# A mixture-of-experts stage whose second part is listed from a graph of tasks

## The chip, the cores and the metric

The kernel runs on one core of a Trainium2 chip. The metric is device time in microseconds (us) of the whole program, the median of several executions. Engines are named as in the profile: PE multiplies matrices, DVE and ACT work on vectors, POOL is GpSimd, SP issues most of the loads. Each engine takes its instructions strictly in the order in which they were written for it; an instruction that waits holds up everything behind it on that engine.

## The reference, cut to what matters

Three layers follow each other. A retention (8 x 8 heads of 576 x 64) gives 4608 tokens of 512 numbers. A dense layer maps them by `h = x @ w_in`, `(h - tanh(h)) @ w_out` with 2048 hidden columns. Then each token goes to one of eight experts, and an expert takes exactly 576 tokens:

```
logits = x @ w_gate
order = np.argsort(-flat)            # all (token, expert) pairs, best first
for idx in order:
    tok, e = int(idx) // E, int(idx) % E
    if assigned[tok] >= 0 or counts[e] >= cap: continue
    assigned[tok] = e; counts[e] += 1
for e in range(E):
    h = np.maximum(x[assigned == e] @ w1[e], 0.0)
    out[assigned == e] = h @ w2[e]
```

## The kernel before, in words

The first part (retention and dense layer, `phase_ab`) is listed by a planner of its own, the class `Tasks`; it ends at about 985 us and is the same in both kernels. The second part, `phase_c`, is what the change rewrites. It runs eight rounds. A round has two halves.

Routing (`route(r)`) finds which expert fills up next and which 576 tokens it gets. It is a long chain of small DVE operations with a small PE product after every few of them: six threshold searches (a compare `cmp`, L839 or L925; a product L930 or L934; `ca` L938; products L949 and L950; a reduce, a transpose, a count `pi` L957 to L960), then `GG` (L969, product L973), `X` and the expert's number `ei` (L985 to L990, products L995 and L996), then places and indices: the scan `sc` L1006, `zl` L1013, `zh` L1014, `b1` L1018 (printed `b`), `A` L1021, `R` (one half on ACT, L1019, one on DVE, L1023), product L1027, `im`, `ix`, product L1045, `idx` L1050. Round r+1 starts from the state that round r leaves: `epen`, `v`, `tpen`, `own`, `rem`.

An expert (`experts(r)`, called E0 to E7 here) gathers its tokens by index on POOL (`xg`, L1097, five tiles), turns them on PE (`tp`, L1112), splits them into a high part `xh` (ACT, L1114) and a low part `xl` (DVE, L1115); both weights are loaded by SP (`ws`, L1063 and L1068) and split in the same way into `w1h`, `w2h` (ACT, L1074) and `w1l`, `w2l` (POOL, L1075). The first layer has eight slices f of 24 PE products (L1158), each slice followed by `hh` (ACT, L1167) and three DVE operations for `hl` (L1171); the two PSUM banks of a slice are free again when these are done, and there are four such banks. The second layer has 112 PE products (L1189) in five token tiles (t0, t4, t1, t2, t3), and per tile an output `o` (ACT, L1197, L1199) that POOL scatters (L1201).

What sets the order of all this: `experts` writes its products one by one and calls `tick` after each pair (`TK1` = 0.24) or each one (`TK2` = 0.213). `tick` moves one clock on and lets three threads (routing, first-layer weights, tokens) write their next piece when the distance that they last yielded has passed. The distances are constants:

```
Y_TR, Y_CA, Y_H, Y_GG, Y_X, Y_Z, Y_R, Y_IX = 2.0, 0.85, 0.5, 2.9, 2.7, 4.2, 1.8, 2.7
YS = 0.82, 0.85
```

Everything between two yields is written in one piece. So `b1` and the ACT half of `R` are written together, whatever ACT has still to do for the first layer; and `w2h` of slice f is written behind `hh` of slice f.

Of the kernel before, what the change touches and what calls it, by code (L numbers as in the profile page):

```python
# [41 lines left out]
def lat(a, b):  # L42

    if a == b:
        return 0.0
    if "dma" in (a, b):
        return 0.9 if a == "dma" else 1.2
    return 0.2 if "tensor" in (a, b) else 0.15

# [23 lines left out]
class Tasks:  # L73
# [17 lines left out]
    def run(self, free):  # L91
# [31 lines left out]
        assert left == 0  # L123

# [607 lines left out]


Y_TR, Y_CA, Y_H, Y_GG, Y_X, Y_Z, Y_R, Y_IX = 2.0, 0.85, 0.5, 2.9, 2.7, 4.2, 1.8, 2.7

YS = 0.82, 0.85
TK1 = 0.24
TK2 = 0.213

# [9 lines left out]
def phase_c(tc, ctx, w1, w2, rtf, rti, rth, rtb, x2d, L, out):  # L749
# [69 lines left out]
    key = SB["key"].bitcast(I32)  # L819

    def best(r):

        V.tensor_reduce(SB["m"], VN[r], axis=AX.X, op=OP.max)
        MT[r] = rt([128, NCOL], F32, "mt")
        V.tensor_tensor(MT[r], SB["m"], tpen, op=OP.min)

    def keys(r):

        n1 = SB["n1"].bitcast(I32)
        HI[r] = rt([128, NCOL], I32, "hi")  # L830
        mb = MT[r].bitcast(I32)
        V.tensor_scalar(n1, mb, c31, c80, op0=OP.arith_shift_right, op1=OP.bitwise_or)
        V.tensor_tensor(key, mb, n1, op=OP.bitwise_xor)
        V.tensor_scalar(HI[r], key, c16, cff, op0=OP.arith_shift_right, op1=OP.bitwise_and)
        compare0(r, HI[r])

    def compare0(r, src):
        CM[r] = rt([128, NCOL, 32], BF16, "cmp32")
        V.tensor_tensor(CM[r], bc(src, 2, 32), bc(SB["s0"], 1, NCOL), op=OP.is_ge)  # L839

    def route(r):


        fast = r < FAST
        q0 = rt([128, NCOL, E], F32, "q0")
        e0 = SB["e0"].rearrange("p (c e) -> p c e", e=E)
        m8 = rt([128, NCOL], F32, "m8")
        P = rt([128, NCOL, E], BF16, "P")
        if r == 0:
            best(0)  # L850
            yield 0.75
            keys(0)
            yield 2.0
        v, m, mt = VN.pop(r), SB["m"], MT.pop(r)

        def proposals():
            V.tensor_tensor(q0, v, bc(m, 2, E), op=OP.is_equal)
            yield 0.5
            V.tensor_tensor(e0, q0, bc(SB["w8"], 1, NCOL), op=OP.mult)
            yield 0.5  # L860
            V.tensor_reduce(m8, e0, axis=AX.X, op=OP.max)
            yield 0.5
            V.tensor_tensor(P, e0, bc(m8, 2, E), op=OP.is_equal)
# [5 lines left out]
        GG = rt([128, NCOL, 2, E], BF16, "GG")  # L869
        gg = SB["gg"].rearrange("p (c a) -> p c a", a=2)  # L870
        if r < E - 1:

            hi = HI.pop(r)
            lo = rt([128, NCOL], I32, "lo")
            hs = SB["hs"]
            lf = rt([128, NCOL], F32, "lf")
            T = pi = None
            for half in range(2):
                src = hi
                if half:  # L880
                    ts = rt([128, 1], F32, "ts")
                    V.tensor_scalar(ts, pi, T, 65536.0, op0=OP.add, op1=OP.mult)
                    V.scalar_tensor_tensor(lf, hs, ts, lo, op0=OP.subtract, op1=OP.add)
                    src = lf
                D = None
                for s, (shift, J) in enumerate(STEPS):
                    if s == 0:
                        if half:
                            compare0(r, src)
                        cmp_ = CM.pop(r)  # L890
                        if fast:

                            if not half:
                                src = rt([128, NCOL], F32, "hf")
                                nc.gpsimd.tensor_copy(out=src, in_=hi)
                            D = fp.tile([128, KC, CAP], F32R, tag="xl", name="D", bufs=2)
                            D = D.rearrange("p k t -> p (k t)")[:, :NCOL * 64].bitcast(F32)
                            D = D.rearrange("p (c j) -> p c j", c=NCOL)
                            nc.gpsimd.tensor_tensor(D, bc(src, 2, 64), bc(F["s2"], 1, NCOL), op=OP.subtract)
                            src = lf if half else hi  # L900
                        if not half:
                            yield from proposals()
                            V.tensor_scalar(lo, key, cff, None, op0=OP.bitwise_and)
                            V.tensor_scalar(hs, hi, 65536.0, None, op0=OP.mult)
                            places()
                    elif s == 2 and fast:
                        cmp_ = rt([128, NCOL, J], BF16, "cmp64")
                        V.tensor_scalar(cmp_, D, T, pi, op0=OP.subtract, op1=OP.is_ge)
                        T2 = rt([128, 1], F32, "T")
                        V.tensor_tensor(T2, T, pi, op=OP.add)  # L910
                        T = T2
                    else:
                        cmp_ = rt([128, NCOL, J], BF16, f"cmp{J}")
                        thr = SB["thr"][:, :J]
                        if s == 1:
                            V.tensor_scalar(thr, F["s1"], pi, None, op0=OP.add)
                            T = pi
                        else:
                            V.tensor_scalar(thr, F["s2"], T, pi, op0=OP.add, op1=OP.add)
                            T = rt([128, 1], F32, "T")  # L920
                            V.tensor_copy(out=T, in_=thr[:, :1])
                        for j in range(0, J, 32):
                            if j:
                                yield 1.3
                            V.tensor_tensor(cmp_[:, :, j:j + 32], bc(src, 2, 32), bc(thr[:, j:j + 32], 1, NCOL), op=OP.is_ge)  # L925
                    yield (1.4 if half == 0 and s == 0 else Y_TR + 1.3) + Y_H * (half == 1 and s == 0)
# [9 lines left out]

# [3 lines left out]
                    yield Y_CA + 0.5 * J / 32  # L940


                    nj, nc_ = J // 32, 1 if fast else 4
                    pd = ps_r(8 * nj * nc_)
                    for i in range(nj):
# [4 lines left out]
                        nc.tensor.matmul(o[:, :E], H16["one"], rn, start=False, stop=True)  # L950
                    dm = rt([128, nj], F32, f"dm{nj}")
# [3 lines left out]
                    if not fast:  # L955
                        d8 = rt([128, nj, E], F32, f"d8{nj}")
                        V.tensor_reduce(d8, pd.rearrange("p (j c e) -> p j e c", j=nj, e=E), axis=AX.X, op=OP.add)  # L957
                    V.tensor_reduce(dm, d8, axis=AX.X, op=OP.max)
                    V.transpose(tr.rearrange("p (i j) -> p i j", j=32), bc(dm, 2, 32))
                    V.scalar_tensor_tensor(tr[:, 1:], tr[:, 1:], 0.0, SB["c"][:, s:s + 1].to_broadcast([128, J - 1]),  # L960
                                           op0=OP.is_ge, op1=OP.mult, accum_out=pi)
            V.tensor_scalar(gg[:, :, 0], lf, T, pi, op0=OP.subtract, op1=OP.is_gt)
            V.tensor_scalar(gg[:, :, 1], lf, T, pi, op0=OP.subtract, op1=OP.is_ge)
        else:
            yield from proposals()
            places()
            for a in range(2):
                V.tensor_scalar(gg[:, :, a], mt, -0.5 * BIG, None, op0=OP.is_gt)
        V.tensor_tensor(GG, bc(P, 2, 2), bc(gg, 3, E), op=OP.mult)  # L969
        yield Y_GG  # L970
# [4 lines left out]
        nc.tensor.matmul(pg[:, :16], H16["one"], rz.rearrange("p a e -> p (a e)"), start=False, stop=True)  # L975
        nn = rt([128, 2, E], F32, "nn")
        fw = rt([128, E], F32, "fw")
        mx = rt([128, 1], F32, "mx")
        V.tensor_reduce(nn, pg.rearrange("p (c a e) -> p a e c", c=12, a=2), axis=AX.X, op=OP.add)
        V.scalar_tensor_tensor(fw, nn[:, 1, :], 0.0, SB["w8"], op0=OP.is_ge, op1=OP.mult)  # L980
        V.tensor_reduce(mx, fw, axis=AX.X, op=OP.max)

        X = rt([128, 2, NCOL], BF16, "X")
        tk = rt([128, NCOL], F32, "tk")
        V.scalar_tensor_tensor(tk, m8, mx, gg[:, :, 0], op0=OP.is_equal, op1=OP.mult)  # L985
        V.scalar_tensor_tensor(X[:, 0, :], own, mx, tk, op0=OP.is_equal, op1=OP.add)
# [9 lines left out]
        nc.tensor.matmul(pt[:, :72], B["tri"], X72, start=True, stop=True)  # L996
        if r < E - 1:
            se = rt([128, E], F32, "se")
            V.tensor_scalar(se, SB["w8"], mx, None, op0=OP.is_equal)
            V.scalar_tensor_tensor(epen, se, -2 * BIG, epen, op0=OP.mult, op1=OP.add)  # L1000
            VN[r + 1] = rt([128, NCOL, E], F32, "v")
            V.tensor_tensor(VN[r + 1], L, bc(epen, 1, NCOL), op=OP.min)
        pos = SB["pos"]
        vd = rt([128, 72], F32, "vd")
        pb = rt([128, NCOL], F32, "pb")
        V.tensor_tensor_scan(sc[:, 1:73], one, pt[:, 72:], 0.0, op0=OP.mult, op1=OP.add)  # L1006
        V.tensor_tensor(pos, pt[:, :72], sc[:, 0:72], op=OP.add)
# [299 lines left out]
```

## Time and profile before

| | |
|---|---|
| median of 3 runs | 1521.57 us (1519.9 to 1521.99) |
| the profiled execution | 1526.22 us, its span 1524.0 us |
| PE busy, share of the span | 1448.0 us, 95% |
| DVE, ACT, POOL busy | 71%, 51%, 36% |
| mean granted PE clock over the span | 0.981 |
| first products of E0 to E7 start at | 1041.55, 1107.28, 1167.51, 1228.89, 1293.21, 1353.10, 1414.21, 1467.45 us |

PE is the engine that sets the time: the span can shrink only where PE stands idle or runs at a lower clock. Its 95% is an average, so the table of stages is read for the stretches where PE was not busy, and the list of waits for what ended the idle time.

### The profile page before, as it was taken

To read this page: it belongs to the slowest core of one execution; us is meant where nothing else is said; L and a number is where in the kernel's file an instruction comes from. 1 tells how busy PE (TensorE), PEld (TensorE's weight loads), DVE (VectorE), ACT (ScalarE), POOL (GpSimd) and SP (SyncE) were. 2 spreads that over 40 slices of the span, in tenths; PEclk is the share of its full clock that TensorE was granted. 3 is DMA by queue.
4 is the path that set the end of the run, shared out by engine and by line. 5 is a ranking of instruction groups with operands and counts; after the bars stand their busy time and mean duration, and the time that the engine had idled before them with its cause. 6 is when DMAs were issued, how large, how long until landed. Compare 5 with 4: busy or idle time off the path is not lost.

```text
span 1524.0 us, 26099 instructions
## 1 busy us (share of the span) xinstructions
PE 1448.0 (95%) x9499; PEld 1271.1 (83%) x9500; DVE 1075.9 (71%) x2683; ACT 779.3 (51%) x1616; POOL 541.6 (36%) x487
## 2 busy tenths in 40 slices
PE   7999999999999999999999999928999999999998
PEld 5788888898989888989888998817788788887987
DVE  5777757787888878787878787777676766766210
ACT  6899965555565646565555555512333323424321
POOL 2555631222221213222212222234535626446442
PEclk9999999999999999999999999959999999999999
DMA  8432132111111111202011100112432433426311
GB/s 280 153 118 93 59 124 80 63 42 63 42 63 43 44 62 38 68 22 84 21 63 42 65 1 21 38 63 83 136 117 81 135 96 103 132 75 198 102 59 39
DMA packets 48609, 122.42 MB, mean 80 GB/s; under 512 B 6624, under 2 KB 13408, under 8 KB 48224
## 3 DMA queue, kind: packets, MB, share of 16 engines
q1 hardware_dynamic: 41184, 99.80, 19.4%
q0 software_dynamic: 6144, 19.93, 4.1%
q8 instruction: 75, 1.23, 0.3%
q10 hardware_dynamic: 1152, 1.02, 0.2%
q14 instruction: 54, 0.44, 0.1%
HBM read 101.85 MB, written 18.87 MB: 79 GB/s over the span
## 4 chain that ended last, share of the span: by engine, by line
PE 75%; ACT 9%; DVE 6%; issue 4%; POOL 3%; DMA 2%; SPq 0%; POOLq 0%; ACTq 0%; DVEq 0%
PE x L490 22%; PE h L427 22%; PE ff L1189 12%; PE ff L1158 11%; PE pb L291 2%; PE pb L358 2%; PE pb L370 1%; ACT wst L213 1%; DMA wst<-in_wio 1%; ACT wst L218 1%; ACT t L440 1%; PE tp L1112 1%; PE pb L306 1%; POOL w2l L1075 1%; ACT S L437 1%
## 5 line engine op out<-in xcount | busy, mean ns | idle before, releaser
L471 POOL TENSOR_TENSOR gl<-t,gh 128x384 fp32r<-128x384 f32 x192 | 197.0, 1026 | 632.8 <-ACT gh L468 563.9
L427 PE MATMUL h<-xh,w0h 128*128 128x384 f32 x704 | 238.5, 339 | 2.0 <-DVE t L457 1.9
L437 ACT ACTIVATE S<-h 128x384 f32<-128x384 f32 x192 | 93.2, 486 | 283.4 <-PE h L427 283.4
L427 PE MATMUL h<-xh,w0l 128*128 128x384 f32 x704 | 236.7, 336 | 0.0
L490 PE MATMUL x<-w1h,gh 128*128 128x512 f32 x576 | 231.2, 401 | 3.2 <-ACT gh L468 2.4
L490 PE MATMUL x<-w1l,gh 128*128 128x512 f32 x576 | 226.7, 393 | 0.2 <-DVE w1l L238 0.2
L490 PE MATMUL x<-w1h,gl 128*128 128x512 f32 x576 | 217.8, 396 | 1.3 <-POOL gl L471 0.8
L451 DVE SCALAR_TENSOR_TENSOR t<-t,S 128x384 f32<-128x384 f32 x192 | 114.2, 595 | 140.7 <-ACT t L440 140.0
L531 DVE SCALAR_TENSOR_TENSOR junk<-x2r,wg 128x512 f32<-128x512 f32 x240 | 167.0, 696 | 5.1
L427 PE MATMUL h<-xl,w0h 128*128 128x384 f32 x704 | 151.6, 336 | 0.3 <-DVE xl L414 0.3
L427 PEld LDWEIGHTS h<-xh,w0h 128*128 128x128 f32 x704 | 131.9, 187 | 11.6 <-DVE t L457 3.5
L1075 POOL TENSOR_TENSOR w2l<-ws,w2h 128x512 fp32r<-128x512 f32 x64 | 82.5, 1290 | 164.5 <-ACT w2h L1074 164.5
L427 PEld LDWEIGHTS h<-xh,w0l 128*128 128x128 f32 x704 | 132.1, 188 | 7.1
L490 PEld LDWEIGHTS x<-w1h,gl 128*128 128x128 f32 x576 | 108.3, 189 | 28.8 <-POOL gl L471 5.7
L1189 PE MATMUL ff<-w2h,hh 128*128 128x512 f32 x320 | 128.1, 400 | 3.1 <-DVE hl L1171 2.0
L490 PEld LDWEIGHTS x<-w1h,gh 128*128 128x128 f32 x576 | 108.1, 188 | 26.5 <-ACT gh L468 3.8
L457 DVE COPY_PREDICATED t<-m,h 128x384 f32<-128x384 uint16 x192 | 114.6, 597 | 21.3 <-ACT m L446 2.6
L1189 PE MATMUL ff<-w2l,hh 128*128 128x512 f32 (+1 forms) x320 | 128.0, 400 | 0.6 <-POOL w2l L1075 0.6
L440 ACT ACTIVATE t<-S,bias 128x384 f32<-128x384 f32 x192 | 118.1, 615 | 17.1 <-POOL gl L471 1.1
L427 PEld LDWEIGHTS h<-xl,w0h 128*128 128x128 f32 x704 | 125.6, 188 | 0.9 <-DVE xl L414 0.9
L490 PEld LDWEIGHTS x<-w1l,gh 128*128 128x128 f32 x576 | 108.3, 188 | 17.7 <-DVE w1l L238 0.5
L1158 PE MATMUL ff<-xh,w1h 128*128 128x288 f32 x512 | 115.4, 304 | 6.3 <-DVE hl L1171 5.5
(212 smaller groups left out, 2936.5 us busy)
## 6 DMA issues: line engine op xcount, KB each, us to landing
ws<-in_w SPq DMA_DIRECT2D x128, 256.0 KB, 2.8
ain<-in_qkv SPq DMA_DIRECT2D x36, 768.0 KB, 4.1
wst<-in_wio SPq DMA_DIRECT2D x32, 512.0 KB, 3.6
x2d<-x2r SPq DMA_DIRECT2D x33, 256.0 KB, 2.0
w1h<-in_qkv SPq DMA_DIRECT2D x12, 192.0 KB, 4.4
w1l<-in_qkv SPq DMA_DIRECT2D x12, 192.0 KB, 3.7
w0h<-in_qkv SPq DMA_DIRECT2D x12, 192.0 KB, 4.6
w0l<-in_qkv SPq DMA_DIRECT2D x12, 192.0 KB, 5.3
```

The source lines that it names most:

```text
L291: nc.tensor.matmul(PSA[k][a][:, chunk(c)], kt[r, chunk(c)], q[r, chunk(c)], start=True, stop=True)
L427: nc.tensor.matmul(h[:, :TB], w[0][f][:, hp, :], x, start=i == 0, stop=i == 11)
L437: nc.scalar.activation(S, h, AF.Square, scale=KSC)
L440: nc.scalar.activation(AT[s][2], AT[s][1], AF.Square, bias=bias[:, 0:1])
L451: nc.vector.scalar_tensor_tensor(t, t, PA - PB * PB / 4, S, op0=OP.add, op1=OP.mult)
L457: nc.vector.copy_predicated(t, m.bitcast(U16), h)
L471: nc.gpsimd.tensor_tensor(G[s][1], TT.pop(s), G[s][0].bitcast(F32), op=OP.subtract)
L490: nc.tensor.matmul(X2[n][i], g[:, i * 128:i * 128 + 128], w, start=(f == 0 and g is gh and w is wh), stop=(f == NF - 1 and g is gl))
L531: nc.vector.scalar_tensor_tensor(j, r, 1.0, wg[e // 4][:, e % 4, :], op0=OP.mult, op1=OP.mult, accum_out=L[:, c, e:e + 1])
L1075: nc.gpsimd.tensor_tensor(l, s, h.bitcast(F32), op=OP.subtract)
L1158: nc.tensor.matmul(ps[u], w[:, k, :], x[:, k, 288 * u:288 * u + 288], start=i == 0, stop=i == 11)
L1189: nc.tensor.matmul(o, h, w, start=f == 0 and i == 0, stop=f == 7 and i == len(prods) - 1, skip_group_check=t == 4)
```

## The change: what it does

A new class `Flow` lists the second part. Every instruction, or small group of them, is a task with an engine, a duration in us, an urgency (the fourth argument, higher first) and the tasks that it has to wait for; buffers are such dependencies too. `Flow.run` steps through the tasks in the order of their planned times, and writes on each engine the most urgent one that is ready. `route` yields one engine and one duration per operation in place of distances. Expert products have urgency 1, routing 3 (on ACT 4, on POOL 6), weights 2 to 4, `xl` 4, `hl` and `xh` 5, `hh` 6. Some statements of `route` stand elsewhere: `epen` and `v` behind the `R` product, `zl` behind `b1`, `lo` and `hs` behind the first searches, and the five that update `tpen`, `own`, `rem` behind `idx`. The first slice of E1 uses the order of products by token halves that only E0 had. No arithmetic is added or taken away.

```
-    def tick(dt):
-        clock[0] += dt
-        for th_ in threads:
-            while th_[1] is not None and th_[0] <= clock[0]:
-                d = next(th_[1], None)
...
+    def run(self, free):
+        while any(self.ready.values()):
+            at = {e: max(free[e], min(t["ready"] for t in ts)) for e, ts in self.ready.items() if ts}
+            e = min(at, key=lambda e: at[e])
+            t = min((t for t in self.ready[e] if t["ready"] <= at[e]), key=lambda t: (-t["w"], t["i"]))
+            self.ready[e].remove(t)
+            free[e] = at[e] + t["us"]
+            self.end[t["name"]] = free[e], e
+            t["emit"]()
...
-        V.tensor_scalar(zl, zi, k31, None, op0=OP.bitwise_and)
         V.tensor_scalar(zh, zi, k5, None, op0=OP.arith_shift_right)
+        yield VE, 0.94
...
         nc.scalar.activation(R[:, :, 1, :], b1, AF.Copy, scale=F["p"])
-        yield Y_Z
+        yield VE, 0.3, None
+        V.tensor_scalar(zl, zi, k31, None, op0=OP.bitwise_and)
+        yield VE, 1.38, None
         V.tensor_tensor(A, bc(zl, 2, 32), bc(F["i32"], 1, NCOL), op=OP.is_equal)
...
+            T.add(("ld", r, i, f), SP, 0.85, 4 - i, lambda f=f: load(r, i, f), ("value", r), gone)
+            T.add(("hi", r, i, f), AE, 0.63, i + 1, lambda f=f: high(r, i, f), (("ld", r, i, f), 2.3), used)
+            T.add(("lo", r, i, f), GE, 1.3, 2 * i, lambda f=f: low(r, i, f), ("hi", r, i, f))
...
+            T.add(("turn", r, t), PE, 0.38, 2, lambda t=t: turn(r, t), (("xg", r, t), 2.3), old)
+            T.add(("xl", r, t), VE, us[1], 4, lambda t=t: turned_low(r, t), ("xh", r, t))
...
+                product(("l1", r, f, a), 0.267, lambda f=f, a=a: first(r, f, a, 2), *deps)
+                T.add(("relu", r, f, u), AE, 0.41, 6, lambda f=f, u=u: relu(r, f, u), ("l1", r, f, 11))
+                T.add(("rest", r, f, i), VE, us, 5, lambda f=f, i=i: rest(r, f, i), ("relu", r, f, min(i, 1)))
...
+                    product(("l2", r, t, f, i), 0.228, lambda t=t, f=f, i=i: second(r, t, f, i), *deps)
```

How the order moves is shown at three places. First PE at the start of E0, behind the warm-up products: `tp` turns token tiles, `rt<-P,cmp` is a search of the next routing round, `ff<-xh` and `ff<-xl` are first-layer products. Before:

```order
L1112 MATMUL tp<-tf,xg 128x128 x4
L949 LDWEIGHTS th
L949 MATMUL rt<-ca,th 128x32
...
L1112 MATMUL tp<-tf,xg 128x128 x8
L930 LDWEIGHTS cmp_10795
L930 MATMUL rt<-P,cmp_10795 128x32
...
L1112 MATMUL tp<-tf,xg 128x128 x4
L949 LDWEIGHTS th
L949 MATMUL rt<-ca,th 128x32
...
L1112 MATMUL tp<-tf,xg 128x128 x4
L1158 MATMUL ff<-xh_10763,w1h_10632 128x288
```

After, at the same place:

```order
L1233 MATMUL tp<-tf,xg 128x128 x4
...
L1005 MATMUL rt<-ca,th 128x32
...
L1233 MATMUL tp<-tf,xg 128x128 x8
L1280 MATMUL ff<-xh_10768,w1h_10647 128x288
...
L1233 MATMUL tp<-tf,xg 128x128 x4
L1280 MATMUL ff<-xh_10768,w1h_10647 128x288
...
L1280 MATMUL ff<-xl_10769,w1h_10647 128x288 x4
L978 LDWEIGHTS cmp_10847
L978 MATMUL rt<-P,cmp_10847 128x32
```

The second search product (`cmp_10795` before, `cmp_10847` after) has moved from ahead of the fourth token tile to behind the twentieth first-layer product, and the fifth token tile from ahead of the first product to behind the eighth.

Second, ACT in E3, where `R` is the half of the routing operand, `hh` the first layer's output, `w1h` the next expert's weights. Before:

```order
L1167 ACTIVATE hh<-ff 128x288 x2
L1074 ACTIVATE w2h_13662<-ws_13495 128x512
L1019 ACTIVATE R<-b_13758,tf 128x36x20
L1167 ACTIVATE hh<-ff 128x288 x2
L1074 ACTIVATE w2h_13768<-ws_13551 128x512
L1167 ACTIVATE hh<-ff 128x288 x2
```

After:

```order
L1206 ACTIVATE w2h_13511<-ws 128x512
L1286 ACTIVATE hh<-ff 128x288 x12
L1206 ACTIVATE w1h_13856<-ws 128x512
L1106 ACTIVATE R<-b_13851,tf 128x36x20
L1314 ACTIVATE o<-ff 128x512
```

`R` stood between the `hh` of two slices; it now stands behind the last `hh` of the expert, and no `w2h` stands between the last six slices' `hh`.

Third, DVE in the first routing round, from `im` to the compare of the next round. Before (the five updates stand ahead of this piece, behind `R`):

```order
L1032 SCALAR_TENSOR_TENSOR tpen<-st,tpen 128x36
L1033 TENSOR_TENSOR m_10366<-m_10366,st 128x36
L1034 TENSOR_TENSOR st<-st,m_10366 128x36
L1035 TENSOR_TENSOR st<-st,nn 128x8
L1038 TENSOR_TENSOR im<-rt,tf 128x160
L1040 TENSOR_REDUCE ix<-im 128x40
L823 TENSOR_REDUCE st<-v 128x36
L825 TENSOR_TENSOR mt<-st,tpen 128x36
L1050 TENSOR_REDUCE idx<-rt 128x5
```

After:

```order
L1122 SCALAR_TENSOR_TENSOR st<-se,st 128x8
L1125 TENSOR_TENSOR v<-L,st 128x288
L1129 TENSOR_TENSOR im<-rt,tf 128x160
L1132 TENSOR_REDUCE ix<-im 128x40
L868 TENSOR_REDUCE st<-v 128x36
L1144 TENSOR_REDUCE idx<-rt 128x5
```

The updates of `tpen`, `own` and `rem` have gone behind `idx`; `epen` and `v`, which stood ahead of the scan, have come to the place behind `R`.

## Rows read from the trace of the kernel before

**Rows 1.** Busy time by stretch: us, then each engine, granted clock, DMA

```profile
1027.75:1041.55 13.80, 9.48 (x56) 5.43 (x55) 9.03 (x26) 4.17 (x7) 12.16 (x11) 0.75 0.49 158
1047.62:1400.00 352.38, 339.87 (x2468) 293.24 (x2467) 249.54 (x761) 120.29 (x253) 175.16 (x151) 0.99 0.36 114
1400.00:1515.00 115.00, 115.00 (x690) 103.21 (x689) 22.85 (x63) 34.34 (x75) 50.14 (x44) 1.00 0.25 81
```

**Rows 2.** Waits of PE from 1047.62 to 1515: total us, times, longest

```profile
PE ff L1158 <- DVE hl L1171: 5.5, 6, 2.0
PE ff L1189 <- DVE hl L1171: 2.0, 2, 1.1
PE tp L1112 <- DVE xl L1115: 1.4, 1, 1.4
PE ff L1189 <- ACT w2h L1074: 1.1, 1, 1.1
PE ff L1189 <- POOL w2l L1075: 0.6, 1, 0.6
```

**Rows 3.** Timeline in E3: start, length, engine, instruction, idle before and releaser

```profile
1254.62 0.91 DVE L1018 TENSOR_TENSOR b<-st,tf 128x720 bf16<-128x720 int32 x1
...
1255.56 0.89 ACT L1019 ACTIVATE R<-b,tf 128x720 bf16<-128x720 bf16 x1 [6.83 <-DVE b L1018]
...
1257.30 1.10 PE L1158 MATMUL ff<-xh,w1h 128*128 128x288 f32 x2 [2.00 <-DVE hl L1171]
```

**Rows 4.** Busy time by stretch, where PE ran at a lower clock

```profile
1080.00:1084.00 4.00, 4.00 (x18) 2.72 (x17) 1.49 (x7) 2.48 (x5) 4.00 (x4) 0.57 0.89 331
1257.00:1262.00 5.00, 4.58 (x21) 4.40 (x22) 3.54 (x8) 1.69 (x5) 2.51 (x2) 0.66 0.85 267
```

**Rows 5.** Timeline at the end of the first routing round

```profile
1018.87 0.14 DVE L990 TENSOR_SCALAR ei<-mx 128x1 int32<-128x1 f32 x1
...
1019.39 0.45 DVE L1002 TENSOR_TENSOR v<-L,st 128x288 f32<-128x288 f32 x1
...
1021.34 0.26 DVE L1013 TENSOR_SCALAR st<-st,ti 128x36 int32<-128x36 int32 x1
...
1024.03 0.90 DVE L1023 TENSOR_TENSOR R<-b,st 128x720 bf16<-128x720 bf16 x1
1024.06 0.88 ACT L1019 ACTIVATE R<-b,tf 128x720 bf16<-128x720 bf16 x1
```

**Rows 6.** Timeline from the third token tile to E0's first slice

```profile
1036.75 0.66 PE L1112 MATMUL tp<-tf,xg 128*128 128x128 f32 x4 [1.97 <-DVE xl L1115]
...
1037.44 0.60 ACT L1114 ACTIVATE xh<-tp 128x512 fp32r<-128x512 f32 x1 [0.98 <-PE tp L1112]
...
1039.20 0.43 PE L930 MATMUL rt<-P,cmp 128*128 128x32 bf16 x9 [1.79 <-DVE cmp L925]
...
1041.55 0.59 PE L1158 MATMUL ff<-xh,w1h 128*128 128x288 f32 x1
...
1046.53 0.61 PE L934 MATMUL rt<-P,cmp 128*128 128x16 bf16 x18 [1.61 <-DVE cmp L925]
```

**Rows 7.** Chain that ended last, where PE ran undisturbed: start, us, what

```profile
1442.12 25.49 PE ff L1189 x112
1467.62 25.58 PE ff L1158 x192
```

**Rows 8.** Timeline of one search step with nothing else on DVE

```profile
1005.98 0.43 PE L930 MATMUL rt<-P,cmp 128*128 128x32 bf16 x9 [2.74 <-DVE cmp L839]
...
1006.68 0.25 PE L949 MATMUL rt<-ca,th 128*128 128x8 f16 x4 [0.28 <-DVE ca L938]
```

**Rows 9.** Timeline of SP's queue: the first weight loads of both kinds

```profile
1020.21 4.07 SPq L1063 DMA_DIRECT2D ws<-in_w  x8
...
1024.46 1.41 SPq L1068 DMA_DIRECT2D ws<-in_w  x3
```

**Rows 10.** DMA traffic from 1020 to 1045 in 40 slices

```profile
GB/s 0 20 170 364 361 246 200 266 367 367 377 354 364 403 403 302 223 262 138 256 164 184 223 249 170 269 26 0 0 0 0 0 0 0 0 0 0 0 0 0
```

More of the change, by code (lines that the diff above doesn't have):

```diff
@@ new lines, in route, with steps, follow @@
+            V.tensor_tensor(m8, m8, gg[:, :, 0], op=OP.mult)
+            yield VE, 0.23, None
+            V.tensor_tensor(own, own, m8, op=OP.add)
+            yield VE, 0.2, None
+            V.tensor_tensor(rem, rem, nn[:, 0, :], op=OP.subtract)
+    T = Flow()
+    T_names = {r: [] for r in range(E)}
+    def steps():
+        for r in range(E):
+            for d in route(r):
+                yield r, d
+    thread = steps()
+    def follow(before):
+        n = next(thread, None)
+        if n is None:
+            return
+        r, (e, us, *deps) = n
+        name, on = (r, f"rt{len(T_names[r])}"), []
+        first = True
+        for d in deps:
+            if d is not None and d[0] == "@":
+                name = r, d[1:]
+            else:
+                first = False
+                if d is not None:
+                    on.append((r, d))
+        if first or e == PE:
+            on.append(before)
+        T_names[r].append(name)
+        T.add(name, e, us, {PE: 3, VE: 3, AE: 4, GE: 6}[e], lambda: follow(name), *on,
+              (before, None) if before else None)
@@ new lines, in tokens, with bank_of, new, first @@
+            T.add(("xl", r, t), VE, us[1], 4, lambda t=t: turned_low(r, t), ("xh", r, t))
+    def bank_of(name, readers):
+        ring.append(readers)
+        return ring[-5] if len(ring) > 4 else []
+    def new(key):
+        PS[key] = psF.tile([128, 512], F32, tag="ff", name="ff")
+    def first(r, f, a, n):
+        if a == 0:
+            new((r, f, 0))
+            new((r, f, 1))
+        xh, xl = XT[r]
+        w1h, w1l = W1[r, f]
+        prods = [(w, xh, k) for k in range(KC) for w in (w1h, w1l)] + [(w1h, xl, k) for k in range(KC)]
+        seq = [(i, u) for i in range(12) for u in range(2)]
+        if f == 0 and r < 2:
+            seq = [(i, u) for p, q in ((0, 8), (8, 12)) for u in range(2) for i in range(p, q)]
+        for i, u in seq[2 * a:2 * a + 2]:
+            w, x, k = prods[i]
+            nc.tensor.matmul(PS[r, f, u][:, :288], w[:, k, :], x[:, k, 288 * u:288 * u + 288], start=i == 0, stop=i == 11)
@@ new lines, in second @@
+    def second(r, t, f, i):
+        if f == i == 0:
+            new((r, t))
+        ps, n = PS[r, t], cut(t)[1]
+        w2h, w2l = (w.rearrange("p k m -> p (k m)") for w in W2[r, f])
+        hh, hl = H[r, f]
+        hh = hh[:, 128 * t:128 * t + 128]
+        if t < 4:
+            o, h, w = ((ps, hh, w2h), (ps, hl[:, 128 * t:128 * t + 128], w2h), (ps, hh, w2l))[i]
+        else:
+            o, h, w = ((ps, hh, w2h), None, (ps[:n], hh[:, :n], w2l))[i]
+        nc.tensor.matmul(o, h, w, start=f == 0 and i == 0, stop=f == 7 and i == 2, skip_group_check=t == 4)
@@ new lines, in scatter, with warm_up, product @@
+    def scatter(r, t):
+        n = cut(t)[1]
+        nc.gpsimd.indirect_dma_start(out=out, out_offset=bass.IndirectOffsetOnAxis(ap=IDX[r][:n, t:t + 1], axis=0),
+                                     in_=O.pop((r, t))[:n], in_offset=None)
+    def warm_up(i):
+        if i == 0:
+            new("warm")
+        nc.tensor.matmul(PS["warm"], B["ones"], tb[:, 256:768], start=True, stop=True)
+    ring, outs, last = [], [], [None]
+    def product(name, us, emit, *deps):
+        T.add(name, PE, us, 1, emit, *deps, (last[0], None) if last[0] else None)
+        last[0] = name
@@ L1223, in phase_c @@
+            old = (outs[-3], 2.2) if len(outs) > 2 else None
+            T.add(("out", r, t), AE, 0.61, 5.5, lambda t=t: result(r, t), ("l2", r, t, 7, 2), old)
+            if t == 4:
+                T.add(("sum", r), VE, 0.7, 5, lambda: total(r), ("out", r, 4))
+            T.add(("sent", r, t), GE, 0.99, 3, lambda t=t: scatter(r, t), ("sum", r) if t == 4 else ("out", r, t))
+            outs.append(("sent", r, t))
+    follow(None)
     for r in range(E):
+        T.add(("value", r), SP, 0.5, 2.5, lambda r=r: value(r), (r, "ei"))
+        weights(r, 1)
+        tokens(r)
+        weights(r, 2)
```

457 lines of the change are left out of this document (254 added, 203 removed).

## The prediction, made before the changed kernel was run

> **What bounds the kernel now.** I read the table of busy time by stretch first. From 1400 to 1515 us PE is busy 115.00 of 115.00 us, from 1047.62 to 1400 only 339.87 of 352.38, and while E0 is being prepared 9.48 of 13.80 [rows 1]. So nothing can be won behind 1400, where routing is nearly over; 12.5 us stand idle in the six experts that share the machine with routing; and some more stand idle ahead of E0. The list of PE's waits says who ended them: `hl`, `w2h`, `w2l` and one `xl` make 10.6 of the 12.5 us [rows 2]. None of these is a slow operation. The timeline shows what they are: in E3 the ACT half of `R` stands in ACT's queue waiting for `b1`, which DVE ends at 1255.5; ACT has then done nothing for 6.83 us, and the `hh` of a finished slice waits behind `R` the whole time. DVE cannot make `hl`, the slice's two PSUM banks stay full, and PE, two slices further, waits 2.00 us [rows 3]. The bound is thus PE plus what an instruction written too early on ACT or DVE does to it.
>
> A second loss shows only in the granted clock. From 1080 to 1084 the mean is 0.57, from 1257 to 1262 it is 0.66 [rows 4]: PE fell from its 2.4 GHz level to 1.2 GHz for some 3 us. Each comes behind idle time of PE: the second behind the 2.00 us just told, the first behind the waits for `w2h` and `w2l` of E0 (1.1 and 0.6 [rows 2]).
>
> **The change, part by part.** All sums are against the profiled execution, 1526.22 us with a span of 1524.0; the median of the runs is 1521.57, 4.65 lower. I form a difference and take it from the median. The work on PE is the same but for its order: a first-layer product costs 25.58 / 192 = 0.133 us and a second-layer one 25.49 / 112 = 0.228 [rows 7], and the list's own 0.267 per pair and 0.228 agree with that.
>
> (a) The end of the first routing round and the preparation of E0. Ahead of `b1` stood `v` (0.45) and `zl` (0.26) [rows 5]. `v` leaves the path altogether, `zl` comes back ahead of `A`, so the DVE half of `R` ends about 0.4 sooner; the ACT half, which ended at the same moment, 1024.94, because two `w1h` were written ahead of it [rows 5], is now the first on ACT and follows `b1`. So `idx` and the gathers come 0.4 sooner, and POOL has time for the third `w1l` that now stands ahead of the gathers. Then the token tiles: PE's third tile waited 1.97 for `xl` [rows 6], since there are two turning banks; that wait stays. Its `xh` ended at 1037.44 + 0.60 = 1038.04, and with it E0's first half of tokens was complete. The products started at 1041.55, because the search product with its 1.79 us wait and the last two tiles stood ahead of them [rows 6]. In the new order one tile, not two, and no search stand there: 3.5 us at most. I take 3.5 + 0.4 = 3.9; if the fourth tile's `xh` (0.60) is needed too and `xl` is later, 2.0; if `xl` of the third tile, now ahead of the transpose and the compare, frees the bank sooner, 5.5.
>
> (b) E0's first slice held a wait of 1.61 for a double compare [rows 6]. In the new order that search stands 58 first-layer products further on (7.7 us), so the wait goes. The fifth tile now stands behind eight products (1.1 us), and its `xh` (0.60) is wanted at once by the other half: I give 0.5 back. Net 1.1, between 0 and 1.6.
>
> (c) The waits from 1047.62 to 1400. `R` now stands behind the last `hh` of its expert, so the six waits for `hl` in the first layer have no cause left; `w2h` and `w2l` of the first expert are split ahead of the second layer instead of behind each slice; `hl` is preferred on DVE to routing. I take the 10.6 us [rows 2], between 0 and the whole 12.5 [rows 1].
>
> (d) The lower clock behind two of these waits: 4 x (1 - 0.57) = 1.7 and 5 x (1 - 0.66) = 1.7 [rows 4]. With the idle time it goes: 3.4, between 0 and 3.4.
>
> (e) New waits. Each of seven rounds has some sixteen PE products of routing that stand in PE's queue whether DVE is ready or not, and everything behind them waits. The tightest distance is from a search product to the `ca` product: 0.70 us when DVE does nothing else [rows 8]. Between the two the new order often has three second-layer products (0.68), besides the nine search products themselves (0.43 at most [rows 8]); so between nothing and 0.4 us is left, and DVE may stand in a compare or in three `hl` operations just then. From below: nothing, since in the trace the second layer's handoffs over similar distances hardly show among PE's waits [rows 2]. From above: one wait like the 1.61 to 1.97 [rows 6] in each of seven rounds, 12.5. I take 4: nearer to the lower row, since routing lies 6 to 8 us of products later behind each expert than before, and so is rarely awaited.
>
> Sum: 3.9 + 1.1 + 10.6 + 3.4 - 4 = 15.0 us less. From the median: 1506.6, rounded to **1506.5**. Moved at no cost: the five updates of `tpen`, `own` and `rem` run while POOL gathers; without that cover, at `zl`'s 0.26 each [rows 5], they would delay the next search by 1.3 us a round, which is inside (e). Behind E6's first slices the order on PE is the same, and the last scatter is untouched.
>
> **A rule that speaks against it.** Eight loads of first weights leave SP within 4.07 us from 1020.21, three of second weights within 1.41 from 1024.46 [rows 9], and five gathers follow; the traffic ends in the 27th of 40 slices of 0.625 us, that is at 1036.9, having peaked at 403 GB/s [rows 10]. So sixteen transfers, issued together, took 16.7 us. The Trainium skill (Trainium Kernel Development and Optimization, Key Constraints) says that DMAs issued from the SP, ACT and POOL queues run on the same 16 DMA engines and interleave. By that rule the list, which gives every load 0.85 us on SP and 2.3 us to land whatever else moves, is too hopeful where it now puts second weights, gathers and scatters together; the rows agree that the pile lasts long, and no row shows who in it is late.
>
> **Rivals.**
> 1. *No new waits at all.* If DVE is always ahead, (e) is nothing: 1521.57 - 19 = 1502.5. For it: from 1047.62 to 1400 DVE is busy 249.54 of 352.38 us [rows 1], so it has time to be early. Against: the thin distances of (e).
> 2. *The waits move.* The 10.6 us come back as many short waits for `cmp`, `ca` and `ix`, because the listed times and the real ones drift apart within a round; (a) and (b) remain: 1521.57 - 5.0 = 1516.5. This is also the case in which the list does not do what it says. For it: 112 handoffs, 0.1 us each are enough.
> 3. *Slower: ACT held by late second weights.* At each start of an expert two or three `w2h` now stand in ACT's queue between or ahead of the `xh` of the next expert; before, none did. If their loads come last in a pile of 16.7 us [rows 10], begun 1.2 us after `ei` (1019.01 to 1020.21 [rows 5, 9]), they land 17.9 us after it; the new order has 12.8 us of products and one tile (0.66 [rows 6]) between `ei` and the first `xh` of E1. So `xh`, and with it PE, is 4.4 us late at six boundaries, 26.4 us: 1521.57 - 19 + 26.4 = 1529. It decides from the point where second weights land later than 13.5 us after `ei`, and makes the kernel slower from 3.2 us late on. Against: they leave SP ninth to eleventh, ahead of the gathers, and eleven loads of 256 KB at the 370 GB/s of the same slices take 7.8 us.
>
> **How the numbers follow.** The forecast (1503 to 1513) 0.55; rival 1 0.15; rival 2 0.17; rival 3 0.08; 0.05 for losses that I do not see, at no change or above. The range takes in rivals 1 and 2 with 2.5 us beyond each, and leaves out rival 3 and the losses: 1500 to 1519. What a measurement of this kernel can tell from no change is about 0.2%, 3 us: faster means under 1518.5. That takes the forecast, rival 1 and most of rival 2: 0.84; no change 0.07, slower 0.09.
>
> **What would show it.** (a) E0's first product 9 to 11 us, not 14, behind the `idx` products. (b) No wait of PE for a compare in E0's first slice, a short one for the fifth tile. (c) ACT's `R` without an `hh` behind it, and no wait of PE's first layer for `hl`. (d) A granted clock of 1.00 from E1 on. (e) PE's waits for `cmp`, `ca`, `ix`, `R` and `GG` together near 4 us. Rival 3 would show as waits of PE for `xh` at each expert's start with ACT waiting for a load ahead of it; rival 2 as more than 10 us of waits for DVE's routing. The forecast is wrong if PE still idles over 8 us between E0's second slice and the end of routing.

## The result and the profile after

The changed kernel takes 1506.94 us (median of 4, 1505.81 to 1509.93), the kernel before, run beside it, 1521.02 (4, 1519.90 to 1521.99): ratio 0.9911, 95% interval 0.9894 to 0.9928. Its profiled execution took 1506.16 us with a span of 1504.4. PE's waits from E0's first product on are two lines, against the six kinds that [rows 2, 6] show:

```profile
PE tp L1233 <- DMA xg<-x2d,idx: 6.3, 3, 4.2
PE ff L1280 <- ACT xh L1242: 0.5, 1, 0.5
```

No wait for `hl`, `w2h`, `w2l`, and none for a handoff of routing. The stretches that answer to [rows 1] and [rows 4] (busy us of PE, PEld, DVE, ACT, POOL, then granted clock, DMA share, GB/s):

```profile
1039.73:1380.00 340.27, 337.94 (x2515) 295.71 (x2514) 251.96 (x772) 124.97 (x250) 173.44 (x152) 1.00 0.36 115
1380.00:1400.00 20.00, 15.83 (x93) 13.76 (x92) 6.22 (x12) 7.50 (x13) 13.74 (x13) 0.91 0.71 224
...
1395.00:1398.00 3.00, 2.61 (x12) 2.61 (x12) 0.69 (x1) 0.88 (x2) 2.37 (x4) 0.50 0.68 208
```

For 340 us PE misses 2.3 us of work; then 4.2 are lost at one place. Its timeline, POOL's rows first, then PE's:

```profile
1380.87 0.99 POOL L1324 DMA_INDIRECT out<-o,idx  x1 [0.17 <-issue]
1381.89 1.30 POOL L1210 TENSOR_TENSOR w1l<-ws,w1h 128x512 fp32r<-128x512 f32 x1
1387.84 0.98 POOL L1324 DMA_INDIRECT out<-o,idx  x1 [4.65 <-DMA ws<-in_w]
1388.84 2.54 POOL L1210 TENSOR_TENSOR w2l<-ws,w2h 128x512 fp32r<-128x512 f32 x2
1391.54 0.99 POOL L1227 DMA_INDIRECT xg<-x2d,idx  x1 [0.16 <-issue]
...
1395.39 1.11 PE L1233 MATMUL tp<-tf,xg 128*128 128x128 f32 x4 [4.17 <-DMA xg<-x2d,idx]
```

Read it backwards. PE waits in E6's first slice for the first gathered tile of E7, an expert that starts 50 us later. A gather takes 3.85 us from its start to the transposes (1391.54 to 1395.39); the list has 1.27 + 2.3 + 0.12 = 3.69 for that (the gather on POOL, its landing, the hop to PE), so its time is about right. The gather started late: `idx` was there at 1386.92, but a scatter stood ahead of it on POOL and was held 4.65 us. The releaser named there is not the true one: every scatter writes `out` and waits for the landing of the scatter before it. That one, issued at 1380.87, took 6.2 us, to 1387.07, and POOL's queue stood 6.60 us in one semaphore wait from 1380.5 on, to the same moment (first line, ns). Over the whole second part the scatters take, least, median and most (second line):

```profile
L1324 POOLq EVENT_SEMAPHORE  x1: 6600/6600/6600, 1380.5 to 1380.5; - x1
...
DMA to landing us min/median/max: 2.6/2.8/6.2
```

The head, which answers to [rows 5, 6] (timeline of ACT and PE):

```profile
1020.95 0.89 ACT L1106 ACTIVATE R<-b,tf 128x720 bf16<-128x720 bf16 x1 [31.99 <-DVE b L1104]
...
1025.74 0.27 PE L1137 MATMUL rt<-ix,tb 128*128 128x10 bf16 x4 [0.89 <-DVE ix L1132]
...
1034.93 0.40 PE L1280 MATMUL ff<-xh,w1h 128*128 128x288 f32 x1
...
1037.17 0.41 PE L1280 MATMUL ff<-xh,w1h 128*128 128x288 f32 x1 [0.47 <-ACT xh L1242]
```

From the `idx` products to E0's first product 9.19 us, where it was 14.31 in the profile of [rows 6] and 12.26 in the second profile of the kernel before (next section).

### The profile page after: what moved, and what is told of

Read it like the earlier page. It is cut to its first block, busy times and chain, and to the rows that moved or that the text cites. A ratio compares the mean times of both kernels' runs of the same rounds, so it can differ in the third digit from the quotient of the medians.

```text
span 1504.4 us, 26073 instructions
## 1 busy us (share of the span) xinstructions
PE 1440.1 (96%) x9499; PEld 1268.7 (84%) x9500; DVE 1072.7 (71%) x2683; ACT 788.4 (52%) x1616; POOL 539.6 (36%) x487
## 5 line engine op out<-in xcount | busy, mean ns | idle before, releaser
L501 DVE TENSOR_TENSOR t<-t,h 128x384 f32<-128x384 f32 x192 | 106.4, 554 | 20.3 <-ACT T L491 1.9
L494 ACT ACTIVATE m<-S,bias 128x384 bf16<-128x384 f32 x192 | 116.0, 604 | 1.5 <-DVE t L505 0.6
```

The source lines that it names most:

```text
L494: nc.scalar.activation(AT[s][4], AT[s][1], AF.Relu, bias=bias[:, 1:2])
L501: nc.vector.tensor_tensor(t, t, h, op=OP.mult)
```

## The experiments

Three groups, each on one chip with its own runs of the kernel before, of median 1520.32, 1521.53 and 1523.30 us; all ratios are to those. The first has R later, R on DVE, the five tiles and the statements, the third the cut tail, the later loads, both together and the changed kernel again, the second the rest. The first theory (A) was the prediction's: `R`, written too early, blocks ACT. The rival (A2): `hl` is late because DVE itself does routing ahead of it.

**The kernel before, once more.** Unchanged.

> The kernel before, unchanged, once more with a profile. Its first profiled execution was 4.65 us over the median. If that excess lay at the head of the second part, this one has 14.5 us from R's products to E0's first product (16.56 then), about 62.7 us in E0 (65.73 then) and no waits for w2h and w2l, at 1519 to 1522. Rival: those are a trait of the kernel and show again.

1520.77 us, one run, span 1518.6. The waits for `hl`, `w2h` and `w2l` come back to the tenth (5.5, 2.0, 1.1, 0.6), so they are the order's. The lower clock behind them doesn't. PE's wait in E3 that answers to [rows 3], and the clock behind it and behind the waits for `w2h` and `w2l` of E0 (the stretches that answer to [rows 4]):

```profile
1252.95 0.76 DVE L1171 SCALAR_TENSOR_TENSOR hl<-ff,hh 128x288 fp32r<-128x288 f32 x2 [1.26 <-ACT hh L1167]
...
1253.46 0.89 PE L1158 MATMUL ff<-xh,w1h 128*128 128x288 f32 x2 [1.99 <-DVE hl L1171]
1253.62 0.22 DVE L1171 SCALAR_TENSOR_TENSOR hh<-ff,hh 128x64 fp32r<-128x64 f32 x1
...
1253.95 0.19 PEld L1158 LDWEIGHTS ff<-xh,w1h 128*128 128x128 f32 x1 [0.30 <-ACT w2h L1074]
...
1076.00:1079.00 3.00, 2.73 (x18) 1.97 (x19) 2.06 (x8) 2.97 (x6) 3.00 (x4) 1.00 1.02 369
...
1255.00:1258.00 3.00, 3.00 (x26) 2.73 (x25) 2.09 (x7) 0.83 (x3) 1.37 (x2) 1.00 0.75 210
```

The same idle time, 1.99 and 2.00 us, stood once ahead of the 1.2 GHz level and once not. R's products to E0's first product took 14.49 us here, 16.56 in the first profile. So the 5 us by which that profile lay above the median were such dips and a slow first round and head; this execution is the fairer one to compare with. Of what was expected, the head's part held; the waits of E0 proved a trait, and E0 took 65.05 us, not 62.7.

The same rows show that a wait for `hl` has two halves. The pair of products writes the slice's two banks. The first product follows DVE's first `hl` operation; the weights of the second are loaded at 1253.95, 0.11 us after DVE's third operation (1253.62 + 0.22), and the list of waits does not count this half. In all six such waits of this profile the load follows the third operation's start by 0.33 us, and the pair takes 0.89 us, where an undisturbed one takes 0.42.

The clock was lower at a third place, E0's first products. Above, the kernel before (this profile), below the changed kernel:

```profile
1038.33:1040.88 2.55, 2.55 (x13) 2.55 (x12) 2.38 (x9) 0.38 (x1) 2.26 (x2) 0.50 0.00 0
...
1034.93:1036.09 1.16, 1.16 (x9) 1.16 (x9) 1.12 (x5) 0.60 (x1) 1.16 (x2) 1.00 0.75 187
```

In all five profiles with the order before, the first four to eleven products of E0 start 0.24 us apart, in all nine with a changed list only the first one does so; then it is 0.13. So this dip goes with the order, unlike the two of [rows 4].

**R written later, in the kernel before.**

```diff
-        nc.scalar.activation(R[:, :, 1, :], b1, AF.Copy, scale=F["p"])
-        yield Y_Z
+        yield 3.0
+        nc.scalar.activation(R[:, :, 1, :], b1, AF.Copy, scale=F["p"])
+        yield Y_Z - 3.0
```

> The kernel before with one edit: the ACT half of R is written 2.5 us of products later (behind the hh pair of one more slice, in most rounds), the rest of the order as it was. Theory A (ACT's queue is blocked by an R written too early): ACT's wait of R for b1, 33 us over seven rounds, falls below 15 us; PE's waits for hl, 7.5 us, fall below 3 us, the lower clock behind the longest goes; time 1513 to 1516 against 1521. Theory B (hl is late because DVE does the routing ahead of it, R on ACT stands there only beside it): the hl waits stay at 6 to 8 us and the time at 1519 to 1523.

1516.25 us, ratio 0.9972 (0.9961 to 0.9983). ACT waits 7.5 us for `b1`, not 33.0, but PE still waits 4.8 us for `hl`: between the two theories, the time too.

**R on DVE, in the kernel before.**

```diff
-        nc.scalar.activation(R[:, :, 1, :], b1, AF.Copy, scale=F["p"])
+        V.tensor_scalar(R[:, :, 1, :], b1, F["p"], None, op0=OP.mult)
```

> The kernel before with one edit: both halves of R are made by DVE, so ACT waits for routing nowhere. Theory A: no wait of ACT for b1, PE's waits for hl below 2 us, at a price of one more DVE operation per round (0.3 to 0.9 us, in the first round on the path of the first gathers); time 1513 to 1516. Theory B: the hl waits stay or grow, since DVE has 8 more operations; time 1520 to 1525.

1516.29 us, ratio 0.9970 (0.9959 to 0.9981). ACT waits for routing nowhere, and yet (PE's waits):

```profile
PE ff L1158 <- DVE hl L1171: 4.1, 6, 1.5
PE ff L1189 <- DVE hl L1171: 1.5, 1, 1.5
```

So 5.6 of the 7.5 us have a cause beside `R` on ACT. Yet the time fell by 4.0 us, near to A's range and outside B's: the waits for `w2h` and `w2l` (1.7) are gone and the one for `xl` has shrunk (1.4 to 0.3), so that of the 10.6 us of [rows 2] 4.7 were `R` on ACT. DVE's timeline ahead of the longest wait that is left shows the other cause; from the first row to the last DVE is never idle, 21 operations, all the tail of one routing round, written as one block:

```profile
1299.96 0.36 DVE L979 TENSOR_REDUCE nn<-rt 128x16 f32<-128x192 f32 x1
...
1304.97 0.91 DVE L1018 TENSOR_TENSOR b<-st,tf 128x720 bf16<-128x720 int32 x1
1305.91 0.41 DVE L1019 TENSOR_SCALAR R<-b,tf 128x720 bf16<-128x720 bf16 x1
```

`hl` of a finished slice follows at 1306.24, 6.3 us after the block's start; its `hh` was there at 1302.5. Two slices on PE last 6.4 us (25.58 / 4 [rows 7]), and two slices later the banks are wanted again. Four of the seven waits, 4.4 of the 5.6 us, stand behind such a block, the other 1.2 behind compares of the searches.

**That tail cut in two** (R on DVE as above, from the second round on).

```diff
+        yield 2.5 if r else 0.0
         V.tensor_tensor_scan(sc[:, 1:73], one, pt[:, 72:], 0.0, op0=OP.mult, op1=OP.add)
...
-        yield Y_Z
+        yield Y_Z - (2.5 if r else 0.0)
```

> The kernel before with R made by DVE (as in the run with R on DVE) and, from the second round on, the 20-operation tail of routing on DVE cut in two: 2.5 us of products lie between ei and the scan, taken from the distance behind R. Theory A2 (hl is late because DVE does the whole tail, 6.3 us, ahead of it): hl waits, 5.6 us with R on DVE alone, fall to 1 to 2.5 us (those behind a double compare stay); time 2 to 4 us below that run, 1512 to 1514.5. Rival (DVE is simply late by then, whatever the order): the waits stay at 5 us or turn into waits for R; 1515 to 1518.

1520.16 us, ratio 0.9978 (0.9966 to 0.9989). PE's waits:

```profile
PE rt L1028 <- DVE R L1024: 5.3, 5, 1.4
...
PE ff L1159 <- DVE hl L1172: 2.3, 5, 0.7
```

`hl` falls to 2.3 as A2 said: no wait stands behind the block any more, all that are left stand behind compares. But the distance that this takes from `R` comes back as 5.3 us of waits for `R`, which is what the rival had named, and the time is above both ranges, no better than without the cut. So this run shows that the block held `hl`, not that DVE had the time to spare. That the changed kernel shows: with DVE as long busy in E0 to E6 (270.72 us against 269.69) it waits neither for `hl` nor for `R`.

What the list makes of the tail is seen on its DVE, here in E4. Two of the three rounds whose tail still meets `hl` have two groups of `hl` in it, one has one; in the first three of these six rounds the whole tail stands behind the expert's last `hl`.

```profile
1298.13 0.76 DVE L1291 SCALAR_TENSOR_TENSOR hl<-ff,hh 128x288 fp32r<-128x288 f32 x2
...
1298.93 0.14 DVE L1077 TENSOR_SCALAR ei<-mx 128x1 int32<-128x1 f32 x1
...
1301.43 0.76 DVE L1291 SCALAR_TENSOR_TENSOR hl<-ff,hh 128x288 fp32r<-128x288 f32 x2 [0.46 <-ACT hh L1286]
...
1302.23 0.90 DVE L1104 TENSOR_TENSOR b<-st,tf 128x720 bf16<-128x720 int32 x1
```

**hl behind routing, in the changed kernel.**

```diff
-                T.add(("rest", r, f, i), VE, us, 5, lambda f=f, i=i: rest(r, f, i), ("relu", r, f, min(i, 1)))
+                T.add(("rest", r, f, i), VE, us, 2, lambda f=f, i=i: rest(r, f, i), ("relu", r, f, min(i, 1)))
```

> The changed kernel with one number changed: on DVE the list prefers routing to hl (urgency of hl 2 in place of 5; routing has 3). Theory A2 (hl is late because of the routing that stands ahead of it on DVE, R on ACT adds to it): PE's waits for hl, none now, come back with 5 us or more and the time is 1510 to 1516. Theory A (R's place on ACT is the cause): R still stands where the list puts it, hl waits below 2 us, time 1505 to 1509.

1554.94 us, ratio 1.0220 (1.0197 to 1.0243): slower by more than the whole gain, but not by the waits that either theory named:

```profile
PE rt L1116 <- DVE R L1112: 12.1, 3, 4.7
PE tp L1233 <- DMA xg<-x2d,idx: 10.8, 8, 4.1
PE rt L978 <- DVE cmp L864: 4.0, 2, 2.1
```

One wait for `hl` came back, of 2.2 us: too much for A, too little for A2. A reading that no run tests is that the list, told that routing comes first, writes routing's products early on PE, and DVE is not there yet. The run shows how much hangs on DVE's order, not which share of (c) it is.

**Five tiles ahead of E0's first product.**

```diff
-                        x = [("xh", r, t) for t in range(5)] if r > 1 else [("xh", r, t) for t in range(3)]
+                        x = [("xh", r, t) for t in range(5)]
```

> The changed kernel with one edit: E0's first product is listed behind all five token tiles, as it stood before, in place of behind three. From the idx products to E0's first product 9.2 us become 12 to 13.5 (two tiles at 0.7 to 1.1 and the compare product's distance), the first slice's wait of 0.5 goes; time 1509 to 1511 against 1507. Rival: E0's weights or DVE's xl set the start anyway, then below 1 us more, 1506 to 1508. The list is made anew from there on, so later waits can differ; the trace's head decides.

1510.21 us, ratio 0.9936 (0.9919 to 0.9952). From the `idx` products (1025.54) to E0's first (1035.75) 10.21 us against 9.19: the two tiles are worth 1.0 us, at the rival's bound. (The edit holds for E1's first product too, and the list behind is another, so the time is not read.)

**The routing statements put back.** `epen`, `v` and `zl` stand where they stood:

```diff
             V.tensor_scalar(se, SB["w8"], mx, None, op0=OP.is_equal)
+            V.scalar_tensor_tensor(epen, se, -2 * BIG, epen, op0=OP.mult, op1=OP.add)
+            V.tensor_tensor(VN[r + 1], L, bc(epen, 1, NCOL), op=OP.min)
...
+        V.tensor_scalar(zl, zi, k31, None, op0=OP.bitwise_and)
         V.tensor_scalar(zh, zi, k5, None, op0=OP.arith_shift_right)
```

> The changed kernel with the moved routing statements put back: the penalty of the expert, v and zl stand ahead of b1 again. From the X products to idx 0.4 to 0.8 us longer in the first round, where DVE has nothing else; in the later rounds nothing that PE waits for; time 1507 to 1508, not to be told from 1507. Rival: DVE has slack there, then idx at the same distance.

1507.84 us, one run. From the X products to the `idx` products 8.22 us (1017.52 to 1025.74), as before (8.23); the changed kernel takes 7.96. So the statements are worth 0.27 us, less than the 0.4 to 0.8 expected.

**The scatter behind the gathers.**

```diff
-            T.add(("sent", r, t), GE, 0.99, 3, lambda t=t: scatter(r, t), ("sum", r) if t == 4 else ("out", r, t))
+            T.add(("sent", r, t), GE, 0.99, 3, lambda t=t: scatter(r, t), ("sum", r) if t == 4 else ("out", r, t),
+                  (("xg", 7, 4), None) if (r, t) == (5, 2) else None)
```

> The changed kernel with one order changed on POOL: E5's fourth scatter stands behind E7's five gathers in place of ahead of them. Theory C (POOL stood 4.65 us at that scatter, which waits for the landing of the scatter before it, 6.2 us instead of 2.8, so the gathers came 4.6 late): the gathers start at idx, PE's wait of 4.17 for E7's first tile falls below 0.6 and the lower clock behind it goes; 1501 to 1503 against 1507. Rival (the gathers themselves land late in the pile of weight loads): the wait stays at 2 us or more, 1504 to 1507.

1504.53 us, ratio 0.9890 (0.9847 to 0.9932). POOL around E6's start, which is at 1393.39:

```profile
1386.33 1.30 POOL L1210 TENSOR_TENSOR w1l<-ws,w1h 128x512 fp32r<-128x512 f32 x1
1388.46 3.79 POOL L1210 TENSOR_TENSOR w2l<-ws,w2h 128x512 fp32r<-128x512 f32 x3 [0.83 <-ACT w2h L1206]
1392.39 0.97 POOL L1227 DMA_INDIRECT xg<-x2d,idx  x1
```

The gather starts 1.00 us ahead of E6, not 2.60 behind it; E6 has no wait and a clock of 1.00 and takes 53.41 us, not 58.92. Theory C holds at its place; the time, with runs from 1498.56 to 1511.97, can't tell it from the changed kernel.

**E7's loads later.** In the last round `ei` is written behind `idx` and a slice of E6:

```diff
         IDX[r] = idx
+        if r == E - 1:
+            yield VE, 0.15, ("rest", 6, 1, 2), "@ei"
+            ei = rt([128, 1], I32, "ei", E)
+            V.tensor_scalar(ei, mx, -1.0, float(E), op0=OP.mult, op1=OP.add)
+            EI[r] = ei
```

> The changed kernel with one edit: E7's number for the loads is written behind E6's second slice, so E7's eight loads of first weights leave SP only then, some 15 us later, and E6's second weights are no longer behind them. Theory D (the scatter that POOL waited for landed after 6.2 us because eleven loads of 256 KB were under way): it lands in 2.6 to 3.5 us, POOL waits at the next scatter below 1.5 us in place of 4.65, PE's wait for E7's first tile falls below 1 us; 1502 to 1505. Rival (scatters land late there for another reason): 5 us or more, the wait stays.

1513.74 us, ratio 0.9940 (0.9923 to 0.9957), in the third group. Without the loads under way the same scatter waits for something else, and less (1.45 us, where the unchanged list waits 4.65 in its first profile and 3.48 on this chip):

```profile
1387.48 0.99 POOL L1330 DMA_INDIRECT out<-o,idx  x1 [0.17 <-issue]
1388.49 1.31 POOL L1216 TENSOR_TENSOR w1l<-ws,w1h 128x512 fp32r<-128x512 f32 x1
1391.24 0.98 POOL L1330 DMA_INDIRECT out<-o,idx  x1 [1.45 <-ACT o L1320]
```

No wait for E7's gathers is left: theory D holds for the wait. How fast the scatter before landed is not measured here, only that 3.76 us were enough (1387.48 to 1391.24). The forecast time was missed; the unchanged list takes 1513.79 us on this chip, and both have more waits there (last section). The Trainium skill (Trainium Kernel Development and Optimization, Key Constraints) says that DMAs from SP, ACT and POOL run on the same 16 DMA engines and interleave; these two runs agree, 6.2 us for a scatter beside the loads and at most 3.76 without them.

**Tiles later in the list.**

```diff
-            T.add(("turn", r, t), PE, 0.38, 2, lambda t=t: turn(r, t), (("xg", r, t), 2.3), old)
+            T.add(("turn", r, t), PE, 0.38, 2, lambda t=t: turn(r, t),
+                  (("xg", r, t), (2.3, 6.0, 6.0, 6.0, 6.0, 6.0, 6.0, 12.0)[r]), old)
```

> The changed kernel with one number changed: the list counts 6 us from a gather to its tile's transposes (12 for E7, 2.3 as before for E0) in place of 2.3. If PE's waits for gathers (6.3 us in the profiled execution, 1.7 more at the lower clock) are only transposes written too early, they go and nothing takes their place: 1498 to 1501. Rival: the tiles then come too late for the experts' starts, and waits for xh take their place: 1504 to 1510.

1504.49 us, ratio 0.9882 (0.9858 to 0.9906). The time is the rival's. Behind E0's preparation no wait for a gather is left, but others are, 4.9 us in place of 6.8, and the clock fell in E1 (0.97):

```profile
PE ff L1280 <- ACT xh L1242: 2.6, 3, 1.9
PE ff L1280 <- DVE hl L1291: 1.4, 1, 1.4
```

**Both together.** The scatter's dependence as above, and for the tiles:

```diff
+                  (("xg", r, t), (2.3, 4.0, 3.5, 3.5, 3.5, 3.5, 3.5, 6.0)[r]), old)
```

> The changed kernel with two edits: the list counts 4.0 us from gather to transposes for E1, 3.5 for E2 to E6 and 6 for E7 (2.3 before; 2.3 stays for E0), and E5's fourth scatter stands behind E7's gathers. If the waits for gathers (6.3 us in the first profile of the changed kernel, 4.6 with the scatter moved alone) are the last thing that PE loses and are only a matter of the listed landing time: below 1.5 us of them, no more than 1.5 us of others, 1499.5 to 1503. Rival (each later tile makes the list's other places worse, as with 6 us): 1503 to 1506.

1515.68 us, ratio 0.9945 (0.9929 to 0.9961), against 0.9933 for the unchanged list on the same chip: a miss of both ranges. The waits for gathers went, others came, 14.6 us with E0's preparation, as many as the unchanged list has there. No version is shown to beat the changed kernel.

**The changed kernel, once more**, on the third chip. Unchanged.

> The changed kernel, unchanged, once more with a profile, to tell what is the kernel's and what one execution's. Expected: PE's waits for gathers again first, 4 to 8 us; the 4.17 us wait for E7's first tile again at 3 to 5 if it is a trait of the order, and the lower clock behind it only perhaps, since in the kernel before the same waits stood once with it and once without; 1505 to 1509.

1513.79 us, ratio 0.9933 (0.9918 to 0.9948); PE's waits from E0's preparation on, 14.6 us together:

```profile
PE rt L1005 <- DVE ca L995: 5.4, 3, 2.6
PE tp L1233 <- DMA xg<-x2d,idx: 5.2, 3, 2.4
PE tp L1233 <- DVE xl L1246: 2.5, 3, 1.2
```

The time is above its range. E7's first tile is waited for again (2.01 us, less than the 3 to 5 expected), with no lower clock behind it. The waits for `ca` are new, and no operation of DVE stands ahead of it in the longest of them (last section).

## Why the prediction was right, point by point

Against the second profile of before, the spans differ by 14.2 us, the timed medians by 14.1. By stage, before to after: first round of routing (first search product to R's products) 30.00 to 29.49; R's products to E0's first product 14.49 to 11.46; E0 to E6 as the sums of seven stretches show, before first; the rest 56.5 in both.

```profile
sum 423.76, PE 409.69 PEld 355.50 DVE 269.69 ACT 142.71 POOL 213.05; mean PE 58.53 PEld 50.79 DVE 38.53 ACT 20.39 POOL 30.44
```

```profile
sum 412.93, PE 405.96 PEld 356.46 DVE 270.72 ACT 150.85 POOL 215.22; mean PE 57.99 PEld 50.92 DVE 38.67 ACT 21.55 POOL 30.75
```

So 3.5 us at the head and 10.8 in the experts, of which 7.1 are idle time and 3.7 shorter busy time. The forecast had 3.9, 7.7 (1.1 + 10.6 - 4) and 3.4 for the three.

- (a) The size holds (3.9 forecast, 3.5 measured), the shares less: the statements 0.27, not 0.4; the tiles 1.0 of the 3.5. The rest, about 2 by subtraction, is put down to the search step that no longer stands ahead of the products with its 1.79 us wait [rows 6]; no run moved it alone. That it stood there was told, that it weighs more than the tiles was not.
- (b) Holds: the compare wait (1.61, in the second profile 0.72) is gone, the fifth tile's 0.47 is there.
- (c) All 10.6 us of waits [rows 2] went, as forecast. The cause told, `R` too early on ACT, was half of it: with `R` off ACT 4.7 of the 10.6 went, and 5.6 of 7.5 us of `hl` waits stayed, most of them behind DVE's block. Even in E3 [rows 3] `hh` did not wait behind `R` for the whole 6.83 us, since PE ended that slice only at 1252.1, and DVE stood still for it 1.26 us, not 2.00. What the list does is to move routing's tail behind the last `hl` or to put `hl` between its operations. The prediction had both, the first in (e), the second in half a sentence of (c), but not that DVE's block was a cause.
- (d) This step failed. The two dips of the clock were put down to the waits ahead of them; with the same waits and no dip in the second profile, they were that execution's. The 3.7 us of shorter busy time come from elsewhere. The second halves of the six waits for `hl` count as busy time, 0.47 us each, 2.8 together, in E1 to E5, which are 3.4 shorter. E0 is 1.9 shorter, 1.3 of it (half of 2.55) for its first products at the 1.2 GHz level. E6 is 1.5 longer, for the lower clock behind E7's tile. So the term's size was right by luck.
- (e) 4 us forecast, 6.3 measured in the first profile (and 1.5 at the lower clock: E6's busy time is 54.75 us, 53.22 before), in the wrong place: waits for gathers, 4.17 of it for one held behind a scatter on POOL, not handoffs of routing. On the third chip the handoffs show too, and there the gain is smaller, 9.5 us.

The sum was made against a profile 4.65 us over the median and taken from the median; the parts of it that were that execution's (the dips, 3.4) and the parts not seen (the shorter busy time, 3.7) about cancelled. Rival 3 didn't show: PE waits for no `xh` at an expert's start but for E0's fifth tile. Its mechanism, transfers late in a pile, did, on another queue: the loads made POOL's scatter late, not ACT's `w2h`.

## What to carry to other kernels

Before a loss is put down to a place, profile the unchanged kernel twice: here the waits that the order made came back to the tenth of a us, and two of the three dips of the clock did not. When a queue is seen waiting, ask whether the engine that it waits for is late by its own order; here ACT waited for DVE's 21-operation block, and with ACT's early `R` gone the block still held `hl`. Look behind a wait, too: the second half of each wait for `hl` counted as busy time. A planner must know every wait and how long it can last: this one did not know that a scatter waits for the landing of the scatter before it, nor that a landing can take 6.2 us, and that was its largest loss left in the first profile (4.17 us). Moving that scatter took the wait away, but no run shows that it makes the kernel faster.

## What the runs showed of the hardware that was not expected

On the third chip the changed kernel's list meets pauses in which PE, DVE and ACT stand still together. PE's products end at 1206.47 and 1206.96, but DVE and ACT, which need only these, start 3 us later (timeline, all engines):

```profile
1206.08 0.39 PE L978 MATMUL rt<-P,cmp 128*128 128x32 bf16 x9
...
1206.32 0.64 PE L1233 MATMUL tp<-tf,xg 128*128 128x128 f32 x4
...
1210.03 0.19 DVE L995 TENSOR_TENSOR ca<-rt,tf 128x32 f16<-128x32 f32 x1 [3.37 <-remote]
1210.09 0.60 ACT L1242 ACTIVATE xh<-tp 128x512 fp32r<-128x512 f32 x1 [4.15 <-remote]
...
1210.28 0.18 PE L1005 MATMUL rt<-ca,th 128*128 128x32 f16 x1 [2.62 <-DVE ca L995]
```

All three runs of changed lists on that chip show such pauses, while gathers are under way: `ca` starts 1.6 us or more behind its search product at three or four places in each, up to 3.6. The order of the kernel before is not free of them: with the cut tail, on the same chip, one `ca` started 1.77 us behind its product (ended at 1094.41), and in the first profile of the kernel before, on another chip, one 1.90 us. PE went on in both.

```profile
1096.18 0.19 DVE L938 TENSOR_TENSOR ca<-rt,tf 128x32 f16<-128x32 f32 x1 [1.57 <-PE ff L1190]
```

In the profiles of changed lists on the other chips no `ca` that has nothing ahead of it on DVE starts more than 1.2 us behind its product. What holds DVE and ACT there, and whether the gathers have a part in it, stays open; no run moved them away.
